# Attention stage of a fused attention, expert and cosine MLP kernel: weight pieces asked for earlier, key-value products written by two engines, logits summed by three tiles

## The chip, the core and the metric

One Trainium2 chip, one core. The metric is the device time of one execution in microseconds (us), the median of three runs where nothing else is said. The engines are PE (TensorE, matmuls, and as PEld its weight loads), DVE (VectorE), ACT (ScalarE), POOL (GpSimd) and SP (SyncE, which here only issues DMAs). A DMA is issued by SP, ACT or POOL, each from its own queue, and moved by the core's 16 DMA engines. An engine carries out its instructions in the order in which they were written; one that waits on a semaphore holds up all behind it.

## The reference, cut to what matters

```python
# q, k, v: (8 batches, 8 heads, 576 tokens, 64), float32
kv = np.einsum('bhsd,bhse->bhde', k, v)               # linear attention: no softmax
out = np.einsum('bhsd,bhde->bhse', q, kv)
x = out / np.sqrt(np.mean(out * out, -1, keepdims=True) + 1e-06) * g_norm
x = x.transpose(0, 2, 1, 3).reshape(4608, 512)
logits = norm(x) @ norm(expert_emb).T / tau           # 8 experts
e = argmax(logits); gate = softmax(logits)[e]
y = gate * (np.maximum(x @ w1[e], 0) @ w2[e])         # w1: 512x1024, w2: 1024x512
h = y @ w_in                                          # 512 -> 2048
out = (h * np.cos(h)) @ w_out                         # 2048 -> 512
```

## The kernel before, in words

**Three stages.** The attention stage (0 to 157 us) turns 4608 tokens into 36 tiles of 128; the expert layers run chunk by chunk over each expert's tokens; the cosine MLP comes last and is the longest. The change touches the first stage and the first steps of the second.

**A tile t.** Nine tiles stand for a pair of batches: four tiles of 128 tokens of each batch (loads `qm`), and a ninth of both remainders of 64 (loads `qr`). The loop `for t in range(NTILE)` writes for each t: `emit_out(t)` (PE multiplies the turned q by the batch's key-value matrix `kvb`, result `po`), `emit_square(t)` (ACT squares `po`: the mark of a tile in the trace), `emit_root(t-1)` (ACT), `q_by_rows` (ACT copies half a batch of q, four and two tiles ahead), `emit_qT(t+2)` (four transposes on PE, one copy on ACT), the pieces of the next batches' key-value work that the table `due` names, the rank matmuls of a group, `emit_x(t)` (DVE finishes tile t-1: its rows `xg` and its eight expert logits), a split of a weight piece if one is due, and a load of a weight piece.

**Key-value work of a batch.** `kv_pair` multiplies k by v, two heads at a time, in PSUM tile `kvp`; after the last pair ACT writes both halves into `kvb`, a 128x4x144 tile whose two 64-column blocks stand on the diagonal and whose off-diagonal blocks are zero. `kv_transpose` turns `kvb` on PE (four transposes) and copies it (`kvs`), and `kv_logits` multiplies it by the scaled expert embeddings `gz`, so that `emit_out` gives the logits beside the output; three `kvb` take turns over the batches.

**Placing.** Three tiles are a group g. `place(g)` is a generator that `advance` steps through between other work: DVE and POOL find each token's expert (`w`, on POOL), POOL adds up counts (`exc`, `run`), PE ranks the tokens with two small matmuls, DVE makes row numbers, and POOL casts them (`pi`) and scatters the group's tokens to `xs` in device memory with three indirect DMAs. After group 7, POOL loads expert 0's first 304 rows (`xr`, `load_x`) for the expert layers; `turn_first` transposes them at the end of tiles 34 and 35, and `layer1` starts behind tile 35.

**Weight pieces.** `load_piece` asks for 512 KB of w1 and w2 (two DMAs on SP), `split_piece` makes of it a high part (ACT) and a low part (DVE) in `ring`. There are four `raw` buffers. The table `FIRST` says for the first eight pieces at the end of which tile they are asked for and split: `20: (0, 25)` is piece 0, asked for in tile 20, split in tile 25.

**Loads.** `load_kv(b)` and `load_q(b)` issue on SP, in tiles 0, 2, 7, 11, 16 and so on; SP's order at the end is k and v of batch 7, q of batch 7 with two remainders, then the pieces. A DMA on SP or ACT takes the next of eight semaphores in program order and waits for the DMA that had it before.

**`none`.** `yT` in device memory holds the expert layers' output; its columns from 304 to 511 are set to zero by four DMAs on ACT's queue, from a tile that POOL clears, in the prologue.

## Time and profile before

| what | value |
|---|---|
| median of 3 runs | 1394.12 us (1389.71 to 1398.73) |
| profiled execution | 1400.33 us, its span 1398.7 us, mean granted clock 0.982 |
| busy in the span | PE 1346.6 us (96%), DVE 1004.5 (72%), ACT 689.3 (49%), POOL 106.6 (8%) |
| DMA over the span | 291.72 MB, mean 209 GB/s |

The profile is of one execution, 6.2 us over the median; times in its rows count from the start of its span. A row of the timeline gives start, duration, engine, line and operation, and in brackets how long the engine stood idle before it and what released it. "PEclk" is the clock that TensorE was granted, as a share of full speed (2.4 GHz), so that 0.50 is 1.2 GHz. The rows that carry the prediction have a section of their own below.

### The profile page before, as it was taken

How to read it: one execution, taken by the hardware profiler on the slowest of the kernel's cores; microseconds unless marked ns; L12 is line 12 of the kernel's file. 1: busy time of each engine (PE TensorE's matmuls, PEld its weight loads, DVE VectorE, ACT ScalarE, POOL GpSimd, SP SyncE). 2: the span in 40 equal slices, each digit the busy share in tenths (PEclk: the TensorE clock that was granted, in tenths of full speed). 3: DMA queues.
4: the chain of work that ended last, by engine and by line, in shares of the span. 5: the costliest groups of instructions: out<-in, count | busy, mean ns of one | idle time of the engine just before them, and what ended most of it. 6: DMA issues, size and time to landing. Idle time of an engine off the chain costs nothing. (4 is left out here: it accounts for less than half of the span.)

```text
span 1398.7 us, 26412 instructions
## 1 busy us (share of the span) xinstructions
PE 1346.6 (96%) x9545; PEld 1251.5 (89%) x9545; DVE 1004.5 (72%) x2311; ACT 689.3 (49%) x1297; POOL 106.6 (8%) x184
## 2 busy tenths in 40 slices
PE   8997799999999999999999999999999999999995
PEld 7886788999999999998888988988998898898894
DVE  1575868898888888659877677676767767677652
ACT  3766444555455454336545454554545455454441
POOL 1243130000000000000010100101001010000101
PEclk9998899999999999999999999999999999999998
DMA  9998477888887786279674655657466475655530
GB/s 275 279 321 242 121 250 205 242 249 236 244 225 236 225 224 212 50 221 335 218 246 159 224 191 190 211 187 234 160 215 214 159 240 185 200 196 188 197 106 33
DMA packets 210209, 291.72 MB, mean 209 GB/s; under 512 B 23468, under 2 KB 117200, under 8 KB 208856
## 3 DMA queue, kind: packets, MB, share of 16 engines
q1 hardware_dynamic: 191112, 243.25, 57.0%
q0 software_dynamic: 7296, 29.45, 6.4%
q10 hardware_dynamic: 11664, 17.26, 4.2%
q8 instruction: 78, 1.28, 0.4%
q14 instruction: 59, 0.48, 0.1%
HBM read 241.42 MB, written 48.47 MB: 207 GB/s over the span
## 5 line engine op out<-in xcount | busy, mean ns | idle before, releaser
L1230 PE MATMUL o<-ring,g 128*128 128x512 f32 x1728 | 414.6, 395 | 0.0
L1230 PEld LDWEIGHTS o<-ring,g 128*128 128x128 f32 x1728 | 319.5, 188 | 72.7
L234 PE MATMUL hps<-xT,ring 128*128 128x304 f32 x1536 | 241.7, 307 | 2.7 <-DVE xT L223 2.7
L251 PE MATMUL y<-h,ring 128*128 128x304 f32 x1536 | 236.1, 303 | 4.5 <-ACT ring L140 3.2
L251 PEld LDWEIGHTS y<-h,ring 128*128 128x128 f32 x1536 | 221.0, 189 | 4.9 <-ACT ring L140 3.4
L234 PEld LDWEIGHTS hps<-xT,ring 128*128 128x128 f32 x1536 | 220.6, 190 | 3.4 <-DVE xT L223 3.4
L1118 ACT ACTIVATE n<-h 128x512 int32<-128x512 f32 x144 | 90.8, 632 | 118.6 <-DVE h L1155 116.0
L1124 ACT ACTIVATE u<-u,half_pi 128x512 f32<-128x512 f32 x144 | 103.4, 719 | 76.3 <-DVE u L1121 75.9
L1155 DVE TENSOR_TENSOR h<-one,p 128x256 f32<-128x256 f32 x144 | 60.6, 421 | 91.9 <-ACT one L1187 89.5
L1160 DVE TENSOR_TENSOR u<-u,h 128x512 f32<-128x512 f32 x144 | 99.6, 692 | 29.3 <-ACT u L1124 29.1
L240 ACT ACTIVATE h<-hps 128x304 fp32r<-128x304 f32 x128 | 53.8, 420 | 118.7 <-PE hps L234 110.1
L141 DVE TENSOR_TENSOR ring<-raw,ring 128x1024 fp32r<-128x1024 f32 x72 | 87.9, 1220 | 25.8 <-ACT ring L140 22.3
L1138 PEld LDWEIGHTS p<-ring,wa 128*128 128x128 f32 x840 | 103.1, 191 | 1.9 <-DVE u L1160 0.4
L1138 PEld LDWEIGHTS p<-ring,wb 128*128 128x128 f32 x840 | 103.2, 191 | 1.7
L1138 PE MATMUL p<-ring,wa 128*128 128x256 f32 x840 | 103.9, 283 | 0.2 <-DMA wa<-ws 0.2
L1138 PE MATMUL p<-ring,wb 128*128 128x256 f32 x840 | 103.7, 282 | 0.0
L1242 POOL DMA_INDIRECT out<-o_sb,perm_i x36 | 36.2, 1006 | 806.0 <-ACT o_sb L1241 626.6
L1169 DVE TENSOR_TENSOR g<-u,g 128x512 fp32r<-128x512 f32 x144 | 92.5, 683 | 0.1
L1121 DVE SCALAR_TENSOR_TENSOR u<-h,n 128x512 f32<-128x512 f32 x144 | 92.5, 682 | 0.0
L241 DVE SCALAR_TENSOR_TENSOR h<-hps,h 128x304 fp32r<-128x304 f32 x128 | 59.8, 467 | 44.2 <-ACT h L240 43.6
L1187 ACT ACTIVATE one<-p 128x256 f32<-128x256 f32 x72 | 27.6, 383 | 114.7 <-PE p L1138 114.7
L1155 DVE TENSOR_TENSOR one<-one,p 128x256 f32<-128x256 f32 x72 | 30.3, 420 | 74.4 <-PE p L1138 74.3
(222 smaller groups left out, 1763.6 us busy)
## 6 DMA issues: line engine op xcount, KB each, us to landing
wa<-ws SPq DMA_DIRECT2D x252, 256.0 KB
wb<-ws SPq DMA_DIRECT2D x252, 256.0 KB
raw<-in_moe_w SPq DMA_DIRECT2D x144, 256.0 KB
ws<-wa SPq DMA_DIRECT2D x56, 256.0 KB
xr<-xs POOLq DMA_DIRECT2D x16, 627.0 KB, 7.9
yT<-yo SPq DMA_DIRECT2D x64, 152.0 KB
km<-in_k SPq DMA_DIRECT2D x8, 1024.0 KB
vm<-in_v SPq DMA_DIRECT2D x8, 1024.0 KB
```

The costliest lines, as they stand in the source:

```text
L141: nc.vector.tensor_tensor(out=w[:, 1], in0=raw, in1=w[:, 0].bitcast(F32), op=ALU.subtract)
L234: nc.tensor.matmul(out=p[:, 0:CH], lhsT=w[:, a, k * 128:(k + 1) * 128], rhs=c["xT"][b_][k], start=(n == 0), stop=(n == 11),)
L241: V.scalar_tensor_tensor(out=lo, in0=p[:, 0:CH], scalar=0.0, in1=hi.bitcast(F32), op0=ALU.max, op1=ALU.subtract)
L251: nc.tensor.matmul(out=c["y"][d][:, 0:CH], lhsT=w[:, a, 512 + d * 128:512 + (d + 1) * 128], rhs=h[b_], start=(f == 0 and i == 0), stop=(f ...
L1118: nc.scalar.activation(out=n, in_=p, func=ACTF.Copy, scale=TURN, bias=0.25)
L1121: V.scalar_tensor_tensor(out=u, in0=p, scalar=TURN, in1=n, op0=ALU.mult, op1=ALU.subtract)
L1124: nc.scalar.activation(out=u, in_=u, func=ACTF.Sin, scale=2 * math.pi, bias=half_pi)
L1138: nc.tensor.matmul(out=out, lhsT=w[:, wi, a, k * 128:(k + 1) * 128], rhs=x[xi][:, b_, k * 256:(k + 1) * 256], start=(n == 0), stop=(n == 5),)
L1155: V.tensor_tensor(out=out, in0=x, in1=y, op=ALU.add)
L1160: V.tensor_tensor(out=u, in0=u, in1=h, op=ALU.mult)
L1169: V.tensor_tensor(out=g_[1], in0=u, in1=g_[0].bitcast(F32), op=ALU.subtract)
L1230: nc.tensor.matmul(out=ob[b][t], lhsT=g_[a][:, t * 128:(t + 1) * 128], rhs=w[:, b_, m * 512:m * 512 + 512], start=(q_ == 0 and m == 0 and ...
```

## The change

Seven edits, all in the attention stage. `FIRST` asks for pieces 0 and 1 in tiles 17 and 18, so ahead of the last q loads, and for the others in tiles 21 to 31; the splits move to tiles 26, 27, 29, 30, 31, 33 and to the steps g = 0 and g = 2 of the expert layers (36 and 38). `kv_pair` has ACT write one compact tile `kvc`, and POOL copies its halves into `kvb`. `kv_transpose` turns two heads' pairs of `kvc` at once, so two transposes take the place of four; `kv_logits` uses 64-column weights, and ACT copies the logits in two pieces. `gz` and `en` are laid out to fit. The sum of the logits over heads runs once for three tiles in place of once a tile. Clearing `none` and its four DMAs move from the prologue to tile 29, behind the split there.

```diff
--- before.py
+++ after.py
@@ -545,8 +545,9 @@
         en = ca.tile([E, DM], F32, name="en")
         es = ca.tile([E, 8], F32, name="es")
         taub = ca.tile([E, 1], F32, name="taub")
-        gz = ca.tile([128, 4, 2, E], F32, name="gz")
+        gz = ca.tile([128, 2, 2, 2, E], F32, name="gz")
         kvb = [ca.tile([128, 4, KVW], F32, name=f"kvb{i}") for i in range(3)]
+        kvc = ca.tile([128, 4, D], F32, name="kvc")
 
         nc.scalar.dma_start(out=embt, in_=emb)
         nc.scalar.dma_start(out=taub, in_=tau.to_broadcast([E, 1]))
@@ -569,10 +570,6 @@
         nc.vector.tensor_scalar(out=tie_a, in0=erow, scalar1=-1.0, scalar2=8.0, op0=ALU.mult, op1=ALU.add)
         nc.vector.tensor_scalar(out=run, in0=erow, scalar1=float(NT // 128), scalar2=None, op0=ALU.mult)
 
-        none = ca.tile([128, 512 - CH], F32, name="none")
-        nc.gpsimd.memset(none, 0.0)
-        for d in range(4):
-            nc.scalar.dma_start(out=yT[d * 128:(d + 1) * 128, CH:512], in_=none)
         nums = ca.tile([128, 4, 9], I32, name="nums")
         nc.gpsimd.iota(out=nums[:, :, 0:8], pattern=[[2 * S, 4], [S, 2], [1, 4]], base=0, channel_multiplier=4)
         for i in range(2):
@@ -622,13 +619,21 @@
                 out=es[:, 5:6], in0=es[:, 5:6], scalar=1e-6, in1=taub, op0=ALU.add, op1=ALU.mult
             )
             nc.vector.reciprocal(out=es[:, 6:7], in_=es[:, 5:6])
-            nc.vector.tensor_scalar(out=en, in0=embt, scalar1=es[:, 6:7], scalar2=None, op0=ALU.mult)
+            for a in range(2):
+                nc.vector.tensor_scalar(
+                    out=en[:, a * 256:a * 256 + 256].rearrange("x (n i e) -> x n i e", n=2, i=2),
+                    in0=embt[:, a * 256:a * 256 + 256].rearrange("x (i n e) -> x n i e", i=2, n=2),
+                    scalar1=es[:, 6:7], scalar2=None, op0=ALU.mult,
+                )
             pe = ps_t.tile([128, 4, 128], F32, name="qTp", tag="qTp")
-            for hp in range(4):
-                nc.tensor.transpose(out=pe[:, hp, 0:E], in_=en[:, hp * 128:(hp + 1) * 128], identity=ident[0:E, 0:E])
+            for j in range(4):
+                nc.tensor.transpose(out=pe[:, j, 0:E], in_=en[:, j * 128:(j + 1) * 128], identity=ident[0:E, 0:E])
             for i in range(2):
                 r = slice(64 * i, 64 * i + 64)
-                nc.vector.tensor_scalar(out=gz[r, :, i, :], in0=pe[r, :, 0:E], scalar1=g2[r], scalar2=None, op0=ALU.mult)
+                nc.vector.tensor_scalar(
+                    out=gz[r, :, :, i, :], in0=pe[r, :, 0:E].rearrange("p (a n) x -> p a n x", a=2),
+                    scalar1=g2[r], scalar2=None, op0=ALU.mult,
+                )
 
 
         kvp_t = {}
@@ -646,31 +651,35 @@
                 for h, o in ho:
                     nc.tensor.matmul(out=o, lhsT=kr[rr, h, r, :], rhs=vr[rr, h, r, :], start=False, stop=(r == 1))
             if hp == 3:
+                nc.scalar.activation(out=kvc, in_=p[:, :, 0:D], func=ACTF.Copy)
                 for n in range(2):
                     r = slice(64 * n, 64 * n + 64)
-                    nc.scalar.activation(out=dst[r, :, n * D:(n + 1) * D], in_=p[r, :, 0:D], func=ACTF.Copy)
+                    nc.gpsimd.tensor_copy(out=dst[r, :, n * D:(n + 1) * D], in_=kvc[r])
 
         kvs_t = {}
 
         def kv_transpose(b):
-            dst = kvb[b % 3]
             p = ps_s.tile([128, 4, 128], F32, name="kvp", tag="kvp")
-            for hp in range(4):
-                nc.tensor.transpose(out=p[:, hp, :], in_=dst[:, hp, 0:128], identity=ident)
-            kvs_t[b] = tp.tile([128, 4, 128], F32, name="kvs", tag="kvs")
-            nc.scalar.activation(out=kvs_t[b], in_=p, func=ACTF.Copy)
+            for a in range(2):
+                nc.tensor.transpose(out=p[:, a, :], in_=kvc[:, 2 * a:2 * a + 2, :], identity=ident)
+            kvs_t[b] = tp.tile([128, 2, 128], F32, name="kvs", tag="kvs")
+            nc.scalar.activation(out=kvs_t[b], in_=p[:, 0:2], func=ACTF.Copy)
 
         def kv_logits(b):
             a = kvs_t.pop(b)
             p = ps_s.tile([128, 4, 128], F32, name="kvp", tag="kvp").rearrange("p c x -> p (c x)")
-            for hp in range(4):
-                nc.tensor.matmul(
-                    out=p[:, hp * 2 * E:(hp + 1) * 2 * E], lhsT=a[:, hp, :],
-                    rhs=gz[:, hp].rearrange("p n x -> p (n x)"), start=True, stop=True,
+            for i in range(2):
+                for n in range(2):
+                    nc.tensor.matmul(
+                        out=p[64 * n:64 * n + 64, i * 2 * E:(i + 1) * 2 * E], lhsT=a[:, i, 64 * n:64 * n + 64],
+                        rhs=gz[:, i, n].rearrange("p i x -> p (i x)"), start=True, stop=True,
+                    )
+            for n in range(2):
+                r = slice(64 * n, 64 * n + 64)
+                nc.scalar.activation(
+                    out=kvb[b % 3][r, :, 128 + n * E:128 + (n + 1) * E],
+                    in_=p[r, 0:4 * E].rearrange("p (c x) -> p c x", c=4), func=ACTF.Copy,
                 )
-            nc.scalar.activation(
-                out=kvb[b % 3][:, :, 128:KVW], in_=p[:, 0:8 * E].rearrange("p (c x) -> p c x", c=4), func=ACTF.Copy
-            )
 
 
         def where(t):
@@ -690,7 +699,7 @@
             nc.scalar.activation(out=s_, in_=p, func=ACTF.Copy)
             qT[t] = s_
 
-        ms_t, po_t = {}, {}
+        ms_t, po_t, zg = {}, {}, {}
 
         def emit_out(t, po):
             j, b, r = where(t)
@@ -740,7 +749,8 @@
             g, i = group_of[t - 1]
             if i == 0:
                 xg[g] = xp.tile([128, GN, XW], F32, name="xg", tag="xg")
-            z = tp.tile([128, H, E], F32, name="z", tag="z")
+                zg[g] = tp.tile([128, GN, H, E], F32, name="z", tag="z")
+            z = zg[g][:, i]
             nc.vector.tensor_tensor(
                 out=z.rearrange("p (c n) x -> p c n x", c=4), in0=po[:, :, 128:KVW].rearrange("p c (n x) -> p c n x", n=2),
                 in1=yb.to_broadcast([128, 4, 2, E]),
@@ -751,8 +761,10 @@
                 out=xg[g][:, i, 0:DM].rearrange("p (c n d) -> p c n d", c=4, n=2),
                 in0=po[:, :, 0:128].rearrange("p c (n d) -> p c n d", n=2), in1=yb.to_broadcast([128, 4, 2, D]), op=ALU.mult,
             )
-            nc.vector.tensor_reduce(out=xg[g][:, i, DM:XZ], in_=z.rearrange("p h x -> p x h"), axis=AX.X, op=ALU.add)
             if i == GN - 1:
+                nc.vector.tensor_reduce(
+                    out=xg[g][:, :, DM:XZ], in_=zg.pop(g).rearrange("p i h x -> p i x h"), axis=AX.X, op=ALU.add
+                )
                 nc.gpsimd.tensor_copy(
                     out=xg[g][:, :, XZ:XW].bitcast(I32),
                     in_=nums[:, g * GN:(g + 1) * GN].rearrange("p (n o) -> p n o", o=1).to_broadcast([128, GN, XW - XZ]),
@@ -887,7 +899,7 @@
                 if r_ == RANK:
                     ranking.append(it)
 
-        FIRST = {20: (0, 25), 21: (1, 26), 22: (2, 27), 23: (3, 28), 25: (4, 30), 26: (5, 31), 27: (6, 33), 28: (7, 35)}
+        FIRST = {17: (0, 26), 18: (1, 27), 21: (2, 29), 22: (3, 30), 25: (4, 31), 27: (5, 33), 29: (6, 36), 31: (7, 38)}
         late = []
         for t in range(NTILE):
             j, b, r = where(t)
@@ -930,7 +942,10 @@
             if t in FIRST:
                 late.append((FIRST[t][1], load_piece(FIRST[t][0])))
             if t == 29:
-
+                none = ca.tile([128, 512 - CH], F32, name="none")
+                nc.gpsimd.memset(none, 0.0)
+                for d in range(4):
+                    nc.scalar.dma_start(out=yT[d * 128:(d + 1) * 128, CH:512], in_=none)
                 kctx.close()
                 rings.append(pool("ring1", 1, bctx, side="right"))
                 P.xr.append(pool("xr1", 1, bctx, side="right"))
```

On SP, the first loads of q and k, as the program before has them (waits in brackets; DMAHW5 and the like are the semaphores that DMAs on SP and ACT take in turn; the same rows stand in both, so each list is given apart):

```order
L521 DMA vr<-in_v 32x8x128 [waits DMAHW1_49]
L514 DMA qm<-in_q 128x8x256 [waits DMAHW5_49]
L514 DMA km<-in_k 128x8x256 [waits DMAHW6_49]
L514 DMA vm<-in_v 128x8x256 [waits DMAHW7_49]
L521 DMA kr<-in_k 32x8x128 [waits DMAHW0_49]
L521 DMA vr<-in_v 32x8x128 [waits DMAHW1_49]
```

and after:

```order
L521 DMA vr<-in_v 32x8x128 [waits DMAHW0_49]
L514 DMA qm<-in_q 128x8x256 [waits DMAHW1_49]
L514 DMA km<-in_k 128x8x256 [waits DMAHW2_49]
L514 DMA vm<-in_v 128x8x256 [waits DMAHW3_49]
L521 DMA kr<-in_k 32x8x128 [waits DMAHW4_49]
L521 DMA vr<-in_v 32x8x128 [waits DMAHW5_49]
```

The order is the same; the wait of the q load is on another semaphore, because the four `none` DMAs took four of them in before. In tiles 16 to 21 SP's rows before are these, from the loads of batch 7 on (`kr`, `vr`, `qr` are the remainders):

```order
L521 DMA kr<-in_k 32x8x128 [waits DMAHW4_49]
L521 DMA vr<-in_v 32x8x128 [waits DMAHW5_49]
L514 DMA qm<-in_q 128x8x256 [waits DMAHW6_49,Activation_49]
L536 DMA qr<-in_q 64x8x64 [waits DMAHW7_49,PE_49]
L536 DMA qr<-in_q 64x8x64 [waits DMAHW0_49]
L129 DMA raw<-in_moe_w 128x4x128 [waits DMAHW1_49]
L133 DMA raw<-in_moe_w 128x512 [waits DMAHW2_49]
L129 DMA raw<-in_moe_w 128x4x128 [waits DMAHW3_49]
L133 DMA raw<-in_moe_w 128x512 [waits DMAHW4_49]
```

and after:

```order
L521 DMA kr<-in_k 32x8x128 [waits DMAHW0_49]
L521 DMA vr<-in_v 32x8x128 [waits DMAHW1_49]
L129 DMA raw<-in_moe_w 128x4x128 [waits DMAHW2_49]
L133 DMA raw<-in_moe_w 128x512 [waits DMAHW3_49]
L129 DMA raw<-in_moe_w 128x4x128 [waits DMAHW4_49]
L133 DMA raw<-in_moe_w 128x512 [waits DMAHW5_49]
L514 DMA qm<-in_q 128x8x256 [waits DMAHW6_49,Activation_49]
L536 DMA qr<-in_q 64x8x64 [waits DMAHW7_49,PE_49]
L536 DMA qr<-in_q 64x8x64 [waits DMAHW0_49]
L129 DMA raw<-in_moe_w 128x4x128 [waits DMAHW1_49]
```

Two pieces (four DMAs) now stand between `vr` and `qm`.

On POOL, around the counts of group 3 while batch 4's products come, before:

```order
L812 DMA xs<-xg,pi 36864x528
L812 DMA xs<-xg,pi 36864x528 [waits DMASW0_49]
L780 TENSOR_TENSOR w<-w,tie 128x24 [waits DVE_49]
L791 COPY exc<-run 128x8
L793 TENSOR_TENSOR exc<-exc,ohc 128x8 [waits DVE_49,Pool_49]
L793 TENSOR_TENSOR exc<-exc,ohc 128x8 [waits Pool_49]
```

and after (`kvb_151` is batch 4's, DMASW are the semaphores of POOL's own DMAs, here of the six scatters of groups 1 and 2):

```order
L824 DMA xs<-xg,pi 36864x528 x2
L792 TENSOR_TENSOR w<-w,tie 128x24 [waits DVE_49]
L657 COPY kvb_151<-kvc 64x4x64 [waits Activation_49]
L657 COPY kvb_151<-kvc 64x4x64 [waits DMASW5_49,DMASW4_49,DMASW6_49,DMASW3_49,DMASW7_49,DMASW0_49,Pool_49]
L803 COPY exc<-run 128x8 [waits Pool_49]
L805 TENSOR_TENSOR exc<-exc,ohc 128x8 [waits DVE_49,Pool_49]
```

Two copies stand now between `w` and `exc`, the second with a wait for six scatters; batch 6 has the same pattern, and for batches 3, 5 and 7 the two copies stand ahead of the copy of `nums` or of a group's `pi`.

On ACT, from the second copy of batch 7's q to tile 30's square, before:

```order
L610 ACTIVATE qa_1968<-qm 128x1024
L690 ACTIVATE qT<-qTp 128x512 [waits PE_49]
L671 ACTIVATE kvb_151<-kvp 128x4x16 [waits PE_49]
L710 ACTIVATE sq<-po 128x512 [waits PE_49]
L716 ACTIVATE y<-ms,lneps 128x8 [waits DVE_49]
L717 ACTIVATE y<-y 128x8 [waits Activation_49]
L690 ACTIVATE qT<-qTp 128x512 [waits PE_49]
L140 ACTIVATE ring_2042<-raw 128x1024 [waits DMAHW2_49,DMAHW1_49]
```

and after:

```order
L607 ACTIVATE qa_1914<-qm 128x1024
L699 ACTIVATE qT<-qTp 128x512 [waits PE_49]
L679 ACTIVATE kvb_151<-kvp 64x4x8 [waits PE_49]
L679 ACTIVATE kvb_151<-kvp 64x4x8
L140 ACTIVATE ring_1940<-raw 128x1024 [waits DMAHW2_49,DMAHW1_49]
L948 DMA yT<-none 128x208 [waits DMAHW3_49,Pool_49]
L948 DMA yT<-none 128x208 [waits DMAHW4_49]
L948 DMA yT<-none 128x208 [waits DMAHW5_49]
L948 DMA yT<-none 128x208 [waits DMAHW6_49]
L719 ACTIVATE sq<-po 128x512 [waits PE_49]
```

The four writes of `none` stand between the last operation of tile 29 and the square of tile 30 (the first L719), and the first of them waits for POOL. There the rows after are:

```order
L822 CAST pi<-pf 128x3 [waits DVE_49]
L824 DMA xs<-xg,pi 36864x528 [waits Pool_49]
L824 DMA xs<-xg,pi 36864x528 x2
L158 DMA xr<-xs 76x2112 [waits DMASW7_49]
L946 MEMSET none 128x208
L158 DMA xr<-xs 76x2112 [waits DMAHW4_49,DMAHW3_49,DMAHW5_49,DMAHW2_49,DMAHW6_49,DMAHW1_49,DMAHW7_49,DMAHW0_49,PE_49]
```

The memset stands behind the first load of `xr`, which waits for a scatter's landing; in before that load and the second one followed each other.

## Rows read from the trace of the kernel before

**Rows 1.** Busy time by stretch; columns: stretch, length, each engine (count), clock, DMA share.
```profile
80.00:100.00 20.00, 18.61 (x252) 16.80 (x252) 13.23 (x56) 13.65 (x34) 8.98 (x22) 1.00 1.10 307
```

**Rows 2.** Busy time by stretch, five microseconds each.
```profile
120.00:125.00 5.00, 0.00 (x0) 0.00 (x0) 0.72 (x1) 1.78 (x4) 0.00 (x0) 0.50 1.08 341
...
155.00:160.00 5.00, 3.67 (x18) 3.44 (x18) 4.40 (x12) 2.98 (x8) 0.00 (x0) 0.50 0.14 43
```

**Rows 3.** Timeline of ACT: start, duration, line, operation, wait before it.
```profile
123.19 1.06 ACT L140 ACTIVATE ring<-raw 128x1024 fp32r<-128x1024 f32 x1 [9.56 <-DMA raw<-in_moe_w]
...
127.41 1.04 ACT L610 ACTIVATE qa<-qm 128x1024 f32<-128x1024 f32 x1
...
137.86 0.60 ACT L710 ACTIVATE sq<-po 128x512 f32<-128x512 f32 x1
```

**Rows 4.** Timeline of SP's queue: the last q loads and raw 0.
```profile
106.57 7.51 SPq L536 DMA_DIRECT2D qr<-in_q  x2
114.14 1.00 SPq L129 DMA_DIRECT2D raw<-in_moe_w  x1
```

**Rows 5.** Timelines of POOL and DVE, from the scatters of group 6 on.
```profile
107.31 0.98 POOL L812 DMA_INDIRECT xs<-xg,pi  x1 [0.30 <-issue]
...
127.40 1.21 DVE L141 TENSOR_TENSOR ring<-raw,ring 128x1024 fp32r<-128x1024 f32 x1
...
127.56 1.11 POOL L796 COPY run_early<-run 128x8 f32<-128x8 f32 x1
...
142.94 0.59 POOL L158 DMA_DIRECT2D xr<-xs  x1 [3.81 <-DMA xs<-xg,pi]
```

**Rows 6.** Timeline of PE at seven places of the stage and behind it.
```profile
111.29 0.96 PE L667 MATMUL kvp<-gz,kvs 128*128 128x16 f32 x8
...
112.33 0.38 PE L802 MATMUL po<-exc,ones 128*128 128x24 f32 x2
...
114.50 0.69 PE L644 MATMUL kvp<-vm,km 128*64 128x64 f32 x16
...
133.76 0.30 PE L801 MATMUL po<-ohc,upper 128*128 128x24 f32 x2
...
151.28 0.77 PE L217 MATMUL kvp<-ident,xr 76*128 76x76 f32 x4 [2.33 <-DMA xr<-xs]
...
157.22 6.96 PE L234 MATMUL hps<-xT,ring 128*128 128x304 f32 x36 [1.33 <-DVE xT L223]
...
198.16 2.09 PE L251 MATMUL y<-h,ring 128*128 128x304 f32 x8 [3.23 <-ACT ring L140]
```

**Rows 7.** Waits of SP, first 30 us: in all, times, longest.
```profile
SPq L514 <- DMA vm<-in_v: 6.9, 1, 6.9
```

**Rows 8.** Timeline of ACT: the second copy of q.
```profile
30.90 1.06 ACT L610 ACTIVATE qa<-qm 128x1024 f32<-128x1024 f32 x1 [4.03 <-DMA qm<-in_q]
```

**Rows 9.** Groups by line, 0 to 160 us: busy, mean ns, idle before.
```profile
L728 DVE TENSOR_REDUCE ms<-sq 128x8 f32<-128x512 f32 x36 | 24.4, 678 | 12.0 <-ACT sq L710 12.0
...
L754 DVE TENSOR_REDUCE xg<-z 128x8 f32<-128x64 f32 x35 | 9.0, 258 | 0.0
...
L667 PE MATMUL kvp<-gz,kvs 128*128 128x16 f32 x64 | 7.9, 255 | 0.0
...
L659 PE MATMUL kvp<-ident,kvb 128*128 128x128 f32 x32 | 5.2, 288 | 0.0
...
L791 POOL COPY exc<-run 128x8 f32<-128x8 f32 x8 | 1.7, 212 | 0.0
```

**Rows 10.** Scatters of two groups (6, then 7): issue to landing.
```profile
DMA to landing us min/median/max: 7.1/7.4/7.7
...
DMA to landing us min/median/max: 3.0/4.1/4.7
```

**Rows 11.** Instructions of the tile none: duration min, median, max, first and last start.
```profile
L575 ACTq DMA_DIRECT2D yT<-none x4: 338/360/477, 6.7 to 9.1; - x4
L573 POOL MEMSET none<- x1: 261/261/261, 1.8 to 1.8; 128x208 f32 x1
```

## The prediction

> **What bounds the kernel now.** I read the page first: PE is busy 96% of the 1398.7 us span, but the change touches only code that runs in the first tenth of it, where PE falls below nine tenths. Everything after tile 36 is a fixed stream of matmuls that starts later or earlier as a whole. So the question is by how many microseconds the start of the expert layers moves. Then I read busy time by stretch. Between 80 and 100 us the DMA engines are the wall (share 1.10, 307 GB/s), with PE nearly full beside them [rows 1]. Between 120 and 125 us PE does nothing and its granted clock is 0.50, the 1.2 GHz level; it is at that level again in 155 to 160 [rows 2].
>
> The timeline names the hole. ACT ends tile 25 at 113.6 and then stands 9.56 us for raw piece 0, whose split is next in its order; q's rows of batch 7 are turned only at 127.41 [rows 3]. SP's queue shows why the piece is late: raw 0 is issued at 114.14, because the two remainder loads of q ahead of it take 7.51 us from 106.57 [rows 4]. After the hole come group 7's rank at 133.76, its scatters, the load of the first expert's rows at 142.94, a wait of 2.33 us for that load, and the first matmul of the expert layers at 157.22 [rows 5, 6].
>
> **The change, part by part.** I follow three points in turn: when q's rows of batch 7 are copied, when group 7 is ranked, when the expert layers start. Gains are negative.
>
> *Start.* SP stands 6.9 us behind vm's landing before a q load [rows 7], and q's second copy is waited for 4.03 us [rows 8], while the four writes of `none` (426 KB) run. Without those writes the semaphore lanes are dealt out differently, and the first q load has no such wait (order of SP). The last of these waits caps what can come back: bounds 0 and 4.03. I take 3.5, near the cap, since both causes are gone.
>
> *Products.* Four transposes become two, and the logits use 64-column weights. The 8 logits records of 255 ns fill 0.96 us, so pipelined records count about half their length; two transposes less of 288 ns are then 0.3 us [rows 6, 9]. Sixteen 64-column product records fill 0.69 us, so eight logits records will fill 0.35: -0.6 [rows 6]. That is 0.9 a batch, 7 us over eight batches; DMA is the wall too, so I count 4 up to tile 25; bounds 0 and 7. ACT's writes get fewer, and I count nothing: PE hides them, and with ACT on the path they would be worth some 0.4 a batch. The reduce over three tiles costs between a small one (258 ns) and one of 512 elements (678), and replaces three small ones, 774: -0.1 to -0.5 a group, on a DVE that is busy 13.23 of 20 us and waits for others; counted as nothing [rows 1, 9].
>
> *POOL copies.* Here a wait is added. The second copy out of kvc waits for every scatter issued so far; for batches 4 and 6 it stands between w and exc (order of POOL), so the rank matmuls wait for landings, and PE's next tile is queued behind them. At batch 6 the last scatter goes at 107.31 and lands 7.4 later [rows 5, 10], at 114.7; with the copy and three small POOL steps exc is there at 115.6, where PE ran that matmul at 112.33 [rows 6]: 3.3 us. Batch 4 is placed alike, 3.3. For batches 3 and 5 the copy stands in front of a group's pi, up to 2.6 together. Sum 9.2. With the 4.1 of group 7's scatters, which land under lighter DMA [rows 10], 3.3 goes from each, so nothing is left. Bounds 0 and 9.2; a PE that stands lets DMA run ahead, so I take 5. A 64x256 copy on POOL is not in the trace. By the nearest rows it costs from 0.21 (128x8) to 1.11 us (the slowest copy there) [rows 5, 9]: 16 of them are 3.4 to 18 us on a POOL that is busy 8.98 of 20 [rows 1], beside the tiles' work.
>
> That slowest copy, 128x8 as well, took 1.11 us at 127.56, while DVE's subtraction of a split, with two SBUF inputs, ran from 127.40 to 128.61 [rows 5]. The Trainium skill has a rule for it, page "SBUF — State Buffer", section "Who interferes with whom": a DVE instruction with two SBUF inputs and a GpSimd instruction that reads SBUF keep each other out for the whole instruction. The trace agrees in this one case. By that rule batch 7's copies may be held by a split, up to 1.2 us. Tile 31 is the first to read batch 7's kvb, so the sum would stay the same.
>
> *First pieces ahead of q 7.* Tile 25 no longer ends in a split. Raw 0 and 1 are issued where qm 7 stood, and q 7 behind them. In the trace q 7's bytes and raw 0's were in by 123.19. Now raw 1 comes ahead too (512 KB at 307 to 341 GB/s: +1.6), qm 7 comes before the 0.26 MB of qr (-0.8), the bytes of `none` are gone (-1.3), and up to 3.5 of the start comes back: qm 7 lands between 119.2 and 124.0, and I take 121.3. ACT reaches the copy without the hole at 117.3 (113.6, tile 26 and its split), changed by -3.5 - 4 + 5: 114.8. So it **waits for q 7**: the hole passes to a new owner and shrinks, and that wait covers the POOL waits; if q 7 were early they would show in full. Copy: 127.41 to 121.3. From the copy to the rank it was 6.35 us at half clock; its idle parts and one of the two kvb writes gone it is 4.3; between them I take 4.7: rank at 126.0.
>
> *`none` at tile 29.* The second added wait. The memset stands on POOL behind the load of xr, and that waits for group 7's scatters: 9.2 us behind the rank (133.76 to 142.94), then 0.59 of issue and 0.26 of memset [rows 5, 6, 11]: rank + 10.0. The four writes stand on ACT ahead of tile 30's square, which came at rank + 4.1 (137.86) [rows 3]. So ACT stands 5.9 us and then issues four DMAs, 1.4 us (338 ns each) to 2.7 (first start to last end) [rows 11]: tile 30's square at rank + 11.4 to 12.7, mean 12.05. Behind it are queued qT, splits and squares of the last six tiles, and PE and DVE wait for these. From there to the expert layers it was 19.4 us (137.86 to 157.22). The wait of 2.33 for xr goes, since xr landed 8.3 after its issue, rank + 17.5, and is wanted 11 us behind tile 30; one of four splits leaves this stretch, -1.1; a new half-clock stretch is likely behind 7 us of idle PE, but 155 to 160 had one, so +0.5. The expert layers start at rank + 28.5, against 23.5: **+5.0**. Bounds: +1, if the scatters land in their quickest 3.0 and the issues hide, and +7, with the longest issue and more half clock.
>
> *Splits 6 and 7* move behind the start of the expert layers (g 0 and 2). PE stands 3.23 us for a split at 198.16, at the end of a chain from DVE through scatters [rows 6]. One more split on ACT and DVE (1.06 and 1.21 us) ahead of that chain: +0.9; bounds 0 and 2.3.
>
> *Sum.* 126.0 + 28.5 = 154.5 against 157.22: -2.7; +0.9: **-1.8 us**. The profiled execution took 1400.33 (6.2 over the median of 1394.12), so its like would be 1398.5, and the median 1394.12 - 1.8 = **1392.3**.
>
> **Rivals.**
> (a) *The hole closes and nothing takes its place.* q 7 lands at 119.2 (-8.2), the rank follows in 4.3 (-2), `none` costs 1, the later split nothing: -9; if q 7 is there before ACT, which comes at 115.4, it is -13. That is 1381 to 1385. For it: with lighter DMA scatters land in 3.0 to 4.7. Against: the copies of batches 4 and 6 wait inside the saturated stretch, and the order on ACT puts tile 30 behind a landing.
> (b) *`none` costs more than the hole: slower.* The place is ACT ahead of tile 30. q 7 lands at 124.0 (-3.4), the rank follows in 6.35, `none` costs 7, the later split 2.3: +5.9, so 1400. It decides from the point where tile 30's delay behind the rank is larger than the copy's gain. For it: no instruction on PE can fill that stretch. Against: four issues in a row may take 1.4.
> (c) *The change doesn't do what it says.* DMA sets the time up to 120 us, raw and q only swap places, what the start and the products give goes into the wait for q 7, and `none` takes the rest: 0 within 1.5, so 1393 to 1396.
>
> **How the numbers follow.** Forecast (-1.5 to -6): 0.42; (a) 0.22; (b) 0.18; (c) 0.18. The forecast's own range is 1388 to 1392.6. For 8 in 10 I keep the forecast and (c) whole, (a) down to 1382 and (b) up to 1399. A measurement of this kernel can tell about 1% (14 us) from no change, since its runs spread over 9 us. Faster by more than that is only the far end of (a), 0.05; slower by more is beyond (b), 0.02; within 1%: 0.93.
>
> **What would show it.** Right: no wait for raw at tile 25; a wait of 3 to 7 us for qm at the copy near 121; POOL's copies of batches 4 and 6 waiting for scatters, and the rank matmuls for POOL; ACT standing some 6 us ahead of tile 30's square; the expert layers starting between 152 and 157. Wrong: q 7 there without a wait, landings of 3 to 4 us in the saturated stretch, the four writes issued without a wait, a clock that stays at 2.4 GHz from 125 us on, or a start of the expert layers outside 148 to 163.

## The result and the profile after

The changed kernel takes **1409.46 us** (median of 6 runs, 1408.51 to 1410.97) against 1394.78 for the kernel before in the same comparison: ratio 1.0102, 95% interval 1.0083 to 1.0121. Forecast were 1392.3, range 1382 to 1399: wrong in direction, and 10.5 us outside the range.

The start of the expert layers shows the whole loss. Timeline of PE in the profile after (1408.51 us, span 1406.9), at the start of the program, where it stands in the stage, at the first matmul of the expert layers, and at the later split; columns as in [rows 6]:

```profile
12.80 1.08 PE L649 MATMUL kvp<-vm,km 128*64 128x64 f32 x16 [3.67 <-DMA vr<-in_v]
...
71.90 2.26 PE L709 MATMUL po<-kvb,qT 128*128 128x144 f32 x8 [2.16 <-DVE nt L595]
...
89.73 0.62 PE L814 MATMUL po<-exc,ones 128*128 128x24 f32 x2 [3.30 <-POOL exc L805]
...
118.65 2.26 PE L709 MATMUL po<-kvb,qT 128*128 128x144 f32 x8 [1.90 <-DVE xg L760]
...
124.08 0.40 PE L814 MATMUL po<-exc,ones 128*128 128x24 f32 x2 [1.47 <-POOL exc L805]
...
136.75 0.40 PE L813 MATMUL po<-ohc,upper 128*128 128x24 f32 x2
...
149.61 1.11 PE L697 MATMUL qTp<-ident,qa 128*128 128x128 f32 x4 [6.81 <-ACT qT L699]
...
164.82 3.61 PE L234 MATMUL hps<-xT,ring 128*128 128x304 f32 x24 [2.20 <-DVE xT L223]
...
206.72 1.51 PE L251 MATMUL y<-h,ring 128*128 128x304 f32 x7 [2.96 <-ACT ring L140]
```

Where [rows 6] have 133.76, 157.22 and 198.16 stand 136.75, 164.82 and 206.72. PE stands three times in tiles 13 to 26 behind a copy of `kvc` on POOL (directly, or through DVE: 2.16, 3.30 and 1.47 us) and 6.81 us ahead of the transposes for tile 32. The stand of 1.90 us at 118.65 is not behind such a copy: DVE waited there for POOL's `w`, which comes behind the issue of three scatters. Behind these stands lies slow PE time; busy time by stretch, columns as in [rows 1]:

```profile
70.00:75.00 5.00, 3.10 (x14) 2.79 (x14) 3.44 (x13) 0.79 (x2) 1.49 (x7) 0.59 1.07 380
75.00:80.00 5.00, 5.00 (x40) 4.76 (x40) 2.06 (x9) 0.89 (x3) 1.22 (x2) 0.50 1.13 239
85.00:90.00 5.00, 1.70 (x19) 1.40 (x17) 2.32 (x8) 2.69 (x7) 1.25 (x6) 0.80 1.07 375
90.00:95.00 5.00, 5.00 (x46) 4.04 (x46) 2.06 (x9) 1.59 (x4) 3.08 (x5) 0.52 1.13 239
...
125.00:130.00 5.00, 5.00 (x63) 4.00 (x59) 1.96 (x10) 2.53 (x5) 3.52 (x6) 0.55 0.32 121
```

The granted clock falls to 0.50 behind the first stand, to 0.52 behind the second and to 0.55 behind the last; in the first profile of before, it was 1.00 from 60 to 120 us. POOL's timeline shows what it waits for: the second copy of batches 3, 4 and 6 (the third wait is named "issue", but ends when group 5's last scatter, issued at 116.13, lands 6.7 us later), then the load of xr and the memset behind it:

```profile
65.52 0.40 POOL L657 COPY kvb<-kvc 64x256 f32<-64x256 f32 x1 [4.10 <-DMA xs<-xg,pi]
...
88.45 0.40 POOL L657 COPY kvb<-kvc 64x256 f32<-64x256 f32 x1 [5.32 <-DMA xs<-xg,pi]
...
122.80 0.40 POOL L657 COPY kvb<-kvc 64x256 f32<-64x256 f32 x1 [5.09 <-issue]
...
145.04 0.60 POOL L158 DMA_DIRECT2D xr<-xs  x1 [2.06 <-DMA xs<-xg,pi]
145.62 0.30 POOL L946 MEMSET none<- 128x208 f32 x1
```

And ACT's timeline: tile 25's square, the copy of batch 7's q (127.41 in [rows 3]), and tile 29, behind which [rows 3] show a square at 137.86 with no wait:

```profile
120.94 0.60 ACT L719 ACTIVATE sq<-po 128x512 f32<-128x512 f32 x1 [3.17 <-PE po L709]
...
133.20 1.04 ACT L607 ACTIVATE qa<-qm 128x1024 f32<-128x1024 f32 x1
...
141.24 1.06 ACT L140 ACTIVATE ring<-raw 128x1024 fp32r<-128x1024 f32 x1
145.95 2.05 ACTq L948 DMA_DIRECT2D yT<-none  x4
148.05 0.60 ACT L719 ACTIVATE sq<-po 128x512 f32<-128x512 f32 x1 [5.75 <-issue]
```

The hole at tile 25 is gone: no row of after waits for a raw piece there, and none for q of batch 7.

### The profile page after: what moved, and what is told of

Same layout as the page of the kernel before. It is cut to its first block, busy times and chain, and to the rows that moved or that the text cites. A ratio compares the mean times of both kernels' runs of the same rounds, so it can differ in the third digit from the quotient of the medians.

```text
span 1406.9 us, 26390 instructions
## 1 busy us (share of the span) xinstructions
PE 1353.1 (96%) x9529; PEld 1254.8 (89%) x9529; DVE 1003.8 (71%) x2288; ACT 686.3 (49%) x1297; POOL 112.4 (8%) x200
## 5 line engine op out<-in xcount | busy, mean ns | idle before, releaser
L1202 ACT ACTIVATE one<-p 128x256 f32<-128x256 f32 x72 | 27.4, 381 | 114.8 <-PE p L1153 114.8
```

## The experiments

The last column is the first matmul of the expert layers in that kernel's profile. Over these and the kernel before, the profiled execution's time less this start is 1241.8 to 1245.2 us, and 1246.3 and 1247.6 in both_warm and first_z_warm: within some microseconds, the stage after it only shifts. Medians of one comparison share the runs of the kernel before; across comparisons these differ by up to 3 us, so small differences there are read from the ratios too.

| kernel | median us | before us | ratio, 95% interval | start us |
|---|---|---|---|---|
| after | 1409.46 | 1394.78 | 1.0102 (1.0083 to 1.0121) | 164.82 |
| upper_on_act | 1398.10 | 1393.63 | 1.0017 (1.0000 to 1.0034) | 155.03 |
| none_back | 1404.89 | 1393.63 | 1.0063 (1.0041 to 1.0085) | 160.80 |
| both_undone | 1396.48 | 1393.63 | 1.0021 (1.0000 to 1.0043) | 152.27 |
| before_first_only | 1391.95 | 1393.63 | 0.9985 (0.9964 to 1.0006) | 150.52 |
| kv_only | 1402.21 | 1393.77 | 1.0057 (1.0034 to 1.0081) | 157.71 |
| none_only | 1400.24 | 1393.77 | 1.0042 (1.0021 to 1.0063) | 157.19 |
| after_fill | 1416.11 | 1393.77 | 1.0140 (1.0086 to 1.0193) | 173.01 |
| none_split | 1395.16 | 1395.64 | 1.0008 (0.9995 to 1.0021) | 155.78 |
| both_warm | 1400.06 | 1395.64 | 1.0041 (1.0022 to 1.0061) | 153.96 |
| first_z_warm | 1396.33 | 1395.64 | 1.0009 (0.9993 to 1.0024) | 148.81 |
| waits_removed | 1392.16 | 1392.62 | 0.9985 (0.9963 to 1.0006) | 151.42 |
| fill_two | 1405.39 | 1392.62 | 1.0090 (1.0068 to 1.0113) | 161.40 |
| kv_on_act | 1394.10 | 1392.62 | 0.9999 (0.9977 to 1.0020) | 150.88 |
| first_z | 1392.90 | 1392.62 | 0.9998 (0.9976 to 1.0019) | 148.66 |

**The two added waits undone, one by one and together.** In upper_on_act the edit to the changed kernel is

```diff
-                for n in range(2):
-                    r = slice(64 * n, 64 * n + 64)
-                    nc.gpsimd.tensor_copy(out=dst[r, :, n * D:(n + 1) * D], in_=kvc[r])
+                nc.gpsimd.tensor_copy(out=dst[0:64, :, 0:D], in_=kvc[0:64])
+                nc.scalar.activation(out=dst[64:128, :, D:2 * D], in_=p[64:128, :, 0:D], func=ACTF.Copy)
```

In the built program the lower copy never waits for scatters.

> The changed kernel, but the upper half of kvc goes into kvb by ACT, straight from PSUM, as before the change; POOL copies the lower half only, and no copy waits for scatters any more. Theory 1 (the added waits of POOL's copies cost some 9 us by tile 18, about half of it as the half clock behind each wait): tiles 14 to 25 come 8 to 10 us earlier than in the changed kernel, the wait for exc is gone, the granted clock stays at 1.00 from 60 to 110 us, and the median falls by 6 to 9 us, to 1401 to 1403; the rest of the loss stays with the writes of none. Theory 2 (the DMA engines set the pace up to 120 us, and the waits of POOL only fill time that DMA wanted anyway): tile 25 moves by less than 3 us and the median by less than 2.

11.4 us came off where 6 to 9 were expected, and tile 25's square moved from 120.94 to 113.81, though 1.7 of these 7.1 us were there at tile 12 already, ahead of the first stand (65.61 against 67.35). The clock did not stay at 1.00: it was 0.68 from 70 to 75 us and 0.66 from 100 to 105. Theory 2 falls: the time that POOL waited was not DMA's anyway.

In none_back the memset and its four writes go back to their old place:

```diff
+        none = ca.tile([128, 512 - CH], F32, name="none")
+        nc.gpsimd.memset(none, 0.0)
+        for d in range(4):
+            nc.scalar.dma_start(out=yT[d * 128:(d + 1) * 128, CH:512], in_=none)
         nums = ca.tile([128, 4, 9], I32, name="nums")
...
             if t == 29:
-                none = ca.tile([128, 512 - CH], F32, name="none")
-                nc.gpsimd.memset(none, 0.0)
-                for d in range(4):
-                    nc.scalar.dma_start(out=yT[d * 128:(d + 1) * 128, CH:512], in_=none)
```

> The changed kernel, with the clearing of none and its four writes back in the prologue. Theory 1 (ACT stands for the memset behind group 7's scatters and for the issues, 7 us): the step of 7 us between tiles 29 and 30 goes, the prologue loses up to 1 us, and the median falls by 4 to 6 us, to 1403.5 to 1405.5. Theory 2 (xr sets the start of the expert layers anyway, so tile 30 may be late): the median falls by less than 2 us.

4.6 us came off, as expected. both_undone has both edits:

> Both of these undone together: upper half of kvc on ACT, none back in the prologue; the earlier pieces, the two transposes, the 64-column logits and the sum over three tiles stay. If the two waits are the whole loss: 12 to 16 us below the changed kernel, 1393 to 1397 or lower, with the hole at tile 25 gone and a wait for q of batch 7 of 3 to 6 us in its place, so 3 to 6 us faster than the kernel before (1389 to 1392). If the early pieces are themselves the loss (q 7 late behind them): slower than the kernel before, 1397 to 1402.

13 us came off, but 2.9 above the kernel before, not below it, remained; in its profile PE had the half clock from 31 to 41 us, and neither raw nor q of batch 7 was waited for, so the expected wait of 3 to 6 us did not come.

**The parts alone on the kernel before.** before_first_only changes one line:

```diff
-        FIRST = {20: (0, 25), 21: (1, 26), 22: (2, 27), 23: (3, 28), 25: (4, 30), 26: (5, 31), 27: (6, 33), 28: (7, 35)}
+        FIRST = {17: (0, 26), 18: (1, 27), 21: (2, 29), 22: (3, 30), 25: (4, 31), 27: (5, 33), 29: (6, 36), 31: (7, 38)}
```

> The kernel before, with the new table of pieces alone. If the hole at tile 25 passes to q 7 and shrinks: 2 to 6 us below the kernel before, 1389 to 1393, a wait for qm at tile 27 of 4 to 7 us. If q 7 behind two pieces is as late as the piece was: no difference within 1.5 us.

1.7 us less, with an interval that reaches 1.0006. The hole at tile 25 is gone here too, but it did not pass to q 7, whose wait is 0.23 us, not 4 to 7:

```profile
122.92 1.06 ACT L610 ACTIVATE qa<-qm 128x1024 f32<-128x1024 f32 x1 [0.23 <-DMA qm<-in_q]
```

kv_only adds the hunks of the change on `gz`, `en`, `kvc`, `kv_pair`, `kv_transpose` and `kv_logits`, and nothing else:

> The kernel before, with the key-value part alone: kvc, POOL's copies, two transposes, 64-column logits; the pieces, none and the sum per tile as before. Theory 1 (POOL's waits for scatters and the half clock behind them): tiles 14 to 25 come 6 to 10 us late, and since the hole at tile 25 (raw asked for at the old place) hides part of that, the median rises by 3 to 8 us, to 1397 to 1402. If the waits are hidden by the hole altogether: within 2 us of the kernel before.

8.4 us more, just over the range. none_only has the change's hunks on `none` alone:

> The kernel before, with none alone moved to tile 29. Theory 1: tile 30 comes 5 to 7 us later behind group 7's rank, less the 2.3 us of the wait for xr and at most 3.5 us of an earlier start: the median rises by 2 to 5 us, to 1396 to 1399. If the earlier start pays for it: within 1.5 us.

6.5 us more, over the range. The earlier start paid for nothing: tile 0's square came at 28.45, tile 1's at 32.05, where the three profiles of before have 25.96 to 29.10 and 31.68 to 34.11. ACT stood 8.78 us ahead of tile 30's square.

**How long the hole is.** Two more profiles of the kernel before, unedited.

> The kernel before, profiled once more: its first profiled execution took 1400.33 us, at the top of what its runs show (1388 to 1400). If the hole at tile 25 was long by that execution's own bad luck (theory: the typical hole is 3 to 6 us shorter, and the median has little to give back), this profile shows a wait for raw 0 well below 9.56 us in an execution well below 1400. If the hole is as long in any execution: 9 to 10 us again, whatever the time.

> The kernel before, a third profile. If the hole at tile 25 is usually about 3 us (as in the second profile, 2.98 at 1393.2 us) and the 9.56 of the first was that execution's own: a wait for raw 0 of 1 to 5 us, no half clock from 120 to 140 us, an execution of 1389 to 1396. If both occur alike: 8 us or more again.

They took 1393.2 and 1402.7 us. Their timelines of ACT at the split of raw 0, where [rows 3] show 9.56; before_p1 first, with tile 25's square ahead of the split and the copy of batch 7's q behind it, then before_p2:

```profile
112.09 0.60 ACT L710 ACTIVATE sq<-po 128x512 f32<-128x512 f32 x1
...
117.64 1.06 ACT L140 ACTIVATE ring<-raw 128x1024 fp32r<-128x1024 f32 x1 [2.98 <-DMA raw<-in_moe_w]
...
121.87 1.04 ACT L610 ACTIVATE qa<-qm 128x1024 f32<-128x1024 f32 x1
```

```profile
124.62 1.06 ACT L140 ACTIVATE ring<-raw 128x1024 fp32r<-128x1024 f32 x1 [6.61 <-DMA raw<-in_moe_w]
```

In before_p1 the clock stayed at 1.00 behind the hole, and the expert layers began 7.7 us earlier than at the 157.22 of [rows 6]:

```profile
120.00:140.00 20.00, 14.38 (x140) 12.56 (x140) 18.99 (x58) 17.94 (x40) 7.79 (x16) 1.00 0.78 245
...
149.51 7.01 PE L234 MATMUL hps<-xT,ring 128*128 128x304 f32 x36 [1.33 <-DVE xT L223]
```

So neither theory holds as put: the hole is not always long, and not usually 3 us either. It differs from execution to execution, and the execution that I summed on had the longest of three. Nor does the hole alone set an execution's time: before_p2 took longest with a hole of 6.61 us, and its tile 25's square came 3.4 us after that of before_p1 (115.44).

**The clock behind the waits.** Both kernels add dummy matmuls to the changed kernel, into columns of `po` that nobody reads; after_fill has 14 and 12 ahead of tiles 13 and 25 and 22 at groups 3 and 6, fill_two the following:

```diff
+            for i in range({13: 9}.get(t, 0)):
+                nc.tensor.matmul(out=cur["po"][:, 2, 160:224], lhsT=ones, rhs=ones[:, 0:64], start=True, stop=True)
             po = ps_o.tile([128, 4, 256], F32, name="po", tag="po")
...
+        FILL.update({3: 20})
...
             nc.tensor.matmul(out=prv, lhsT=upper, rhs=ohc, start=True, stop=False)
+            if g in FILL:
+                for i in range(FILL[g]):
+                    nc.tensor.matmul(out=cur["po"][:, 2, 160:224], lhsT=ones, rhs=ones[:, 0:64], start=True, stop=True)
```

> The changed kernel, with dummy matmuls on PE (128x64, into unused columns) where it stands for POOL: 14 ahead of tile 13's products, 12 ahead of tile 25's, and 22 between the two rank matmuls of groups 3 and 6. They add work and take no wait away. If half the loss is the clock that falls behind these waits: the granted clock stays near 1.00 from 70 to 100 us, tiles 18 and 24 come 3 to 5 us earlier than in the changed kernel, and the median falls by 2 to 5 us. If only the waits count: no gain, or 1 to 2 us slower.

It lost 6.7 us: at group 6 PE was at the half clock already, and 22 dummies took 9.63 us there, so the median is no test of the question. Ahead of that the clock stayed at 1.00 from 60 to 110 us, and tile 18's square came 2.4 us earlier than in the changed kernel (94.86 against 97.28), tile 24's 0.5 (115.53 against 115.98), where 3 to 5 were expected. The smaller one is:

> The changed kernel with dummy matmuls only at its first two standstills (9 of 128x64 ahead of tile 13's products, 20 between the rank matmuls of group 3), sized from the waits of the changed kernel; the first such kernel had them at group 6 too, where they took 9.6 us at the half clock. If the half clock behind POOL's waits is a part of the loss of its own: clock 1.00 from 70 to 100 us, tiles 14 to 18 come 2 to 4 us earlier than in the changed kernel, and the median falls by 1 to 4 us, to 1405 to 1408. If the next wait takes all of it: tiles 14 to 18 earlier, the median within 1 us of 1409.5.

4.1 us came off by the medians, 1.7 by the ratios, whose intervals overlap, and 3.4 by the start of the expert layers, although work was added. Busy time by stretch in fill_two and, behind it, in after:

```profile
60.00:80.00 20.00, 18.51 (x224) 16.30 (x224) 12.88 (x50) 12.29 (x31) 8.06 (x21) 1.00 1.09 332
80.00:100.00 20.00, 17.68 (x215) 15.42 (x214) 9.89 (x38) 9.64 (x26) 7.68 (x20) 1.00 1.10 307
...
60.00:80.00 20.00, 16.75 (x161) 14.89 (x158) 11.53 (x45) 8.52 (x24) 7.06 (x18) 0.77 1.09 317
80.00:100.00 20.00, 16.33 (x196) 13.78 (x196) 9.94 (x39) 11.18 (x28) 8.09 (x19) 0.80 1.11 311
```

Clock 1.00 in place of 0.77 and 0.80; the wait for POOL is filled, not removed. Tile 14's square came 2.1 us earlier (77.67 against 79.80), but tile 18's only 1.3 (95.97 against 97.28), and tile 24's 0.6 later (116.55 against 115.98); counted from tile 12's, ahead of the first stand, the lead is 2.0 us at tile 18 and 0.2 at tile 24. What is left at the expert layers arose behind tile 24, where fill_two had the higher clock too (0.91 against 0.78 from 120 to 140 us). So the half clock behind the first two stands cost the next tiles some 2 us, and that was gone by tile 24; that it is a part of the kernel's loss is not shown.

**What makes the wait of none.** none_split, on the kernel before, leaves the memset in the prologue and moves the four writes alone:

```diff
         nc.gpsimd.memset(none, 0.0)
-        for d in range(4):
-            nc.scalar.dma_start(out=yT[d * 128:(d + 1) * 128, CH:512], in_=none)
...
             if t == 29:
+                for d in range(4):
+                    nc.scalar.dma_start(out=yT[d * 128:(d + 1) * 128, CH:512], in_=none)
```

> The kernel before with only the four writes of none moved to tile 29; the memset stays in the prologue, so that the writes wait for nothing on POOL. If ACT's stand for the memset behind the scatters is the price of moving none (theory 1): the 6.5 us that moving all of it cost shrink to the issues, 1.4 to 2.7 us, so 1394.5 to 1397. If the four issues and their traffic cost the most: 1398 or more.

The median lies in the first range, 0.5 us under that of the kernel before; by the ratio it is 1.1 above it, with an interval from 0.7 below to 2.9 above. No loss can be told here, so most of the 6.5 us goes with the memset's place behind the load of xr; the issues may keep up to 2.9. The writes themselves are issued beside ACT's work; timeline of ACT and its queue in none_split:

```profile
134.81 1.04 ACT L608 ACTIVATE qa<-qm 128x1024 f32<-128x1024 f32 x1
134.91 0.85 ACTq L932 DMA_DIRECT2D yT<-none  x2
135.76 0.58 ACT L688 ACTIVATE qT<-qTp 128x512 f32<-128x512 f32 x1
135.80 0.58 ACTq L932 DMA_DIRECT2D yT<-none  x1
...
137.02 0.60 ACT L708 ACTIVATE sq<-po 128x512 f32<-128x512 f32 x1 [0.57 <-issue]
```

**Is that the whole loss?** Two runs meant to explain the 2.9 us of both_undone by the clock in tile 2, with eight dummies in tile 1 (first_z_warm has them on the kernel before with the new table and the sum over three tiles):

```diff
+            if t == 1:
+                for i in range(8):
+                    nc.tensor.matmul(out=po[:, 2, 160:224], lhsT=ones, rhs=ones[:, 0:64], start=True, stop=True)
             if t + 2 < NTILE:
```

> The changed kernel with both added waits undone (upper half of kvc on ACT, none in the prologue) and eight dummy matmuls of 128x64 where PE stands 2.5 us for the second q copy in tile 1, ahead of the transposes for tile 3. In the profile without them PE fell to the half clock from 31 to 41 us and tile 2 came 3 us late. If that explains why both_undone stays 2.9 us above the kernel before: clock 1.00 there, tile 2 near 35.5, median 1391 to 1394. If the rest of the key-value part is the reason: no change, 1396 to 1397.

> The kernel before with the new table of pieces, the sum over three tiles, and the same eight dummy matmuls in tile 1; the key-value part and none as before. Expected the fastest: 1388 to 1392, 2 to 5 us below the kernel before, if the table alone gives 1.7 and the clock in tile 2 some 2 more in the executions where it falls; within 1.5 us of the table alone (1392) if the clock there rarely falls.

Both missed: by the ratios 3 us slower than without the dummies (1.0041 against 1.0021 of both_undone), and 1.5 (1.0009 against 0.9998 of first_z, below), neither clear of the intervals. The dummies write the tile that ACT's square reads and waited for it (3.1 us in the profile of both_warm), so they came too late to fill anything. waits_removed settles it another way: the upper copy as in upper_on_act, the memset as in none_split, all else as changed.

> The changed kernel with everything it moves kept, but with what makes the two added waits taken away: the upper half of kvc goes into kvb by ACT, and the memset of none is back in the prologue while its four writes stay at tile 29. If the two waits are the whole loss: the expert layers start within 3 us of the kernel before's shorter profile (149.5), so 147 to 153, and the median is 1390 to 1397. If something else in the change costs: 1398 or more.

17.3 us below the changed kernel (16.3 by the ratios), and the kernel before within the interval. kv_on_act is kv_only with both halves written by ACT from PSUM, as the kernel before does:

> The kernel before with the key-value part alone (kvc, two transposes, 64-column logits), but ACT writes both halves of kvb from PSUM as before, so POOL copies nothing. If the wait of POOL's upper copy is what the key-value part costs: 6 to 9 us below the same with POOL's copies (1402.2), so 1391 to 1396. If kvc, the transposes and the logits in two pieces cost by themselves: 1397 or more.

8.1 us below kv_only. first_z has neither part:

> The kernel before with the new table of pieces and the sum over three tiles, nothing else. The table alone gave 1391.95; the sum over three tiles saves at most 0.5 us of DVE a group, which waits for others: 1390 to 1393.5, 0.5 to 4 us below the kernel before.

Equal to the kernel before. So the two waits are the loss, and the rest of the change gives nothing that can be measured here; no version tried beats the kernel before clear of its interval. Why both_undone stands 2.9 us above it, and waits_removed doesn't, stays open; the two differ only in the place of the four writes, prologue or tile 29.

## Why the prediction was wrong

The miss is 17.2 us (1409.5 against 1392.3). In starts of the expert layers it is 18.0, which two things make up (the 0.9 more is the forecast's term for splits 6 and 7, which lies behind that start; before_p1, the base here, is 0.9 us under its median, the profile after 1.0 under its own).

**The sum's base, 7.7 us.** The prediction subtracted from a start at 157.22 and then carried the difference over to the median, taking the 6.2 us between that execution and the median for something that lies elsewhere. Against before_p1 it lay in the very term that the change was to gain: the hole was 9.56 us with the half clock behind it in that execution, 2.98 without it in one of 1393.2 us. Against that start, 149.51, even my own forecast of 154.5 would have been a loss of 5. The step "Sum" failed there, and with it "copy: 127.41 to 121.3": in before_p1 that copy is at 121.87.

**The changed kernel itself, 10.3 us.** The expert layers start at 164.82, not 154.5.

- *POOL copies* is the step that failed most. The waits were at the places named, and the standing of PE has the forecast size (3.30 us at group 3; 1.47 at group 6, where PE itself was late; 2.16 at batch 3 and nothing at batch 5, for which the prediction put 2.6 without a working). Mis-sized was the price: bounds 0 and 9.2, and I took 5 because a standing PE lets DMA run ahead. The scatters that were waited for still landed 6.7 to 7.6 us after issue (medians of a group's three), and each stand put PE at 1.2 GHz for the tiles behind it, which had no term at all, though the same trace shows it behind the hole [rows 2]. Alone, the part cost 8.4 us (kv_only), and 8.1 of them went with the POOL copies (kv_on_act); in the changed kernel, taking the wait away brought 11.4 (upper_on_act), over my upper bound. How much of that is clock stays open: fill_two shows some 2 us of it at tile 18 and nothing left at tile 24.
- *The cover was not there.* I let a wait for q 7 hide the POOL waits. Tile 25's square came at 120.94, some 9 us after the 112.09 of before_p1, so q 7 was there first and the waits showed in full, with another half-clock stretch behind group 6: the copy came at 133.20, not 121.3. Nor would it have been there without POOL's waits: with the early pieces and no such wait, q 7 is waited for 0.23 us in before_first_only and not at all in first_z, both_undone and waits_removed. In before_first_only it landed at 122.9, inside my 119.2 to 124.0; what was wrong is ACT's 114.8, since in these four ACT reaches the copy at 122.3 to 125.3. The 7.5 us that start and products were to bring ahead of it did not come, and tile 25's square is at 113.34 to 116.82, where the three profiles of before have 111.06 to 115.44; why these tiles come later stays open.
- *Start:* -3.5 forecast, next to nothing found: at tile 12, ahead of the first stand, the changed kernel is 0.5 to 0.8 us ahead of the three profiles of before (67.35 against 67.86, 68.14 and 68.04), what the products gave included. The order of SP showed that the q load no longer waits for vm; it also showed vr's wait on another semaphore, and I read only q's row. vr now waits for km and is issued at 6.45 in place of 3.97; the first product waits 3.67 us for it at 12.80, and tile 0's square comes 2 us later, tile 1's 0.4 earlier, than in the first profile of before. That the new wait loses something is not shown, since tile 0's square is at 28.33 here and at 25.96 to 29.10 in the three profiles of before.
- *Products:* -4 forecast up to tile 25, nothing measured. kv_on_act, which has them without POOL's copies, is at 0.9999 (0.9977 to 1.0020), and its tile 25's square at 114.85 lies within the 111.06 to 115.44 of before, not 4 us ahead of them.
- *`none`* was right in mechanism and nearly in size: ACT stands 5.75 us, the 2.05 of the four issues included, where 5.9 and 1.4 to 2.7 of issues were forecast; tile 30's square comes 11.3 behind the rank (12.05 forecast), and from group 7's rank to the expert layers it is 28.1 us (136.75 to 164.82), where 28.5 was forecast. Alone it costs 6.5, and 4.6 in the changed kernel (none_back).
- *Splits 6 and 7:* right. From the start of the expert layers to the later stand it is 41.9 us (164.82 to 206.72) against 40.9: +1.0, forecast +0.9.

Rival (b) had the direction, with 1400 and a chance of 0.18, and its place (ACT at tile 30) was right; it left POOL's copies out. The chance of 0.02 for slower by over 1% treated the two new waits as never both in full, while the gain against them had been read from the longest hole.

The rule of the Trainium skill (page "SBUF — State Buffer", section "Who interferes with whom") changed no sum, as said; no split held batch 7's two copies, which took 0.84 us together at 135.33. The trace after has a second case of the rule: a POOL addition of 128x8 took 1.20 us at 130.74, where its like take 0.21, and DVE's subtraction of a split ran from 130.66 to 131.87.

## What to carry to other kernels

Before a gain is summed from one stall in one profile, take the profile again: if the execution stands apart from the median, the difference may be that stall. A wait that is added to an engine in the middle of a dense PE stage can cost its length and half-clock time behind it, so price both, from the clock rows behind stands of like length. Here the clock fell behind stands of PE of 2.16 and 3.30 us, and stayed at 1.00 behind one of 2.32 at 31.84 in before_p1. And read every row of the order whose wait changed, not only the one that is meant to improve; a memset or copy queued behind a transfer's landing hands that landing to every engine that waits for it.

## What the runs showed that was not expected

The kernel before is itself uncertain: 31 runs of one comparison lie between 1387.97 and 1401.44 us, and its three profiles show a hole of 9.56, 2.98 and 6.61 us. The changed kernel, which has no such hole, stayed within 2.5 us over 6 runs. That the hole makes the spread is not shown: before_first_only has none either, and its 10 runs lie between 1387.22 and 1396.84. Four DMAs issued by ACT hold up ACT's next square by 0.57 us when nothing holds them and their issue runs beside ACT's work (none_split), and by 5.75, of which 2.05 is the issue, when the first has to wait. And a copy on POOL of the lower 64 partitions carried no wait for POOL's scatters, while that of the upper 64 carried all of them; why the program is built so was not tried.
